# Two attention branches with a gate: a new layout table, later queueing of the local branch's value lists, and a shorter head

## The chip, the cores and the metric

The kernel runs on one core of one Trainium2 chip. The metric is the device time of one execution in microseconds; the time before is 808.96 us, the median of three runs (808.18 to 810.17). A core has five engines with queues of their own: TensorE (PE) multiplies, VectorE (DVE) and GpSimd (POOL) work on tiles, ScalarE (ACT) evaluates functions, and SyncE (SP) issues nearly all transfers here. PEld is TensorE's weight load.

## The reference

Both branches read the same x of 2048 tokens by 640, with 32 heads of 20. Branch A is full softmax attention, branch B attends to 8 positions at a distance of 2 (0, 2, ... 14 tokens back). A gate g per token mixes them.

```python
    def _A_ref(x, wqkv, wo):
        ...
        scores = jnp.einsum("bhqd,bhkd->bhqk", q, k) * scale
        p = _softmax(scores, axis=-1)
        o = jnp.einsum("bhqk,bhkd->bhqd", p, v)
        return (lambda x, *d: x.transpose(*d))(o, 0, 2, 1, 3).reshape(B, S, D) @ wo

    def _B_ref(x, wqkv, wo):
        ...
        W, dil = 8, 2
        ...
        logits = jnp.einsum("bhsd,bhswd->bhsw", q, kg) * scale
        logits = jnp.where(mask[None, None, :, :], logits, -1e9)
        attn = _softmax(logits, axis=-1)
        o = jnp.einsum("bhsw,bhswd->bhsd", attn, vg)
        ...
    x = A_x
    g = _sigmoid((x * gate_w).sum(-1, keepdims=True))
    a = _A_ref(x, A_wqkv, A_wo)
    b = _B_ref(x, B_wqkv, B_wo)
    return g * a + (1 - g) * b
```

## The kernel before

**Main work.** Branch A's scores are computed in units: one head, 128 keys, 512 queries. Four heads form a quad, and a quad with 512 queries is a group; there are 32 groups of 64 units, 2048 in all. PE writes a score tile of two or three units into one of two PSUM banks (line 1672), ACT takes the exponential of the whole tile (line 1697: `ebuf<-score`, 1024 or 1536 columns), and PE multiplies it with the values (line 1742, `obank<-ebuf,vA`). Of some tiles a further unit rides along: DVE turns it into an integer form (line 1687, `uD<-score`), adds three shifts to it (line 899, `eD<-uD`), and PE multiplies the four versions with scaled values (`obank<-uD,vA`, `obank<-eD,vS`). The exponentials of those units are so approximated without ACT: 408 of 2048 units ride, 1640 go through ACT. Each group is closed by a transpose on DVE (line 845, `oTt<-obank`), a division on GpSimd (lines 851 and 858) and a transfer into the layout of the output projection (line 864).

**Side work** goes through spare PSUM banks between the score tiles (helper `mm_group`, line 651): the value projection of A (`gen_v`, copies at line 814), the K and Q projections of the later quads (`gen_kq` in five parts f, `gen_q1` for the first quad), branch B in eight units u of 256 tokens (`gen_bproj` projects Q, K and V, line 945; `gen_b` forms the products and sums, lines 971, 981, 1068, 1078), and the output projection (`gen_fold`). K and Q of `gen_kq` go to the layout of the scores by transfers from `stg` (lines 703, 733, 756). For B, V's shifted windows are copied by four groups of four transfers, the value lists `vR` (line 953, `stage<-qkvB`), which the second product of `gen_b` reads (line 1068); the reciprocal goes through `rB` (lines 1054, 1056).

**The order is set while the program is built.** Every operation is handed to a planner (`T`, class `_Sched`) with an assumed duration and, for transfers, an assumed time to issue (`iss`, times `nd` transfers) and to land. The planner keeps a clock for each engine, and generators yield requests ("dve", "pe", "act", "bank", "cond") that it grants when its clocks allow. What comes out is a fixed order of instructions for each engine and semaphore waits between them; the assumed times are in no instruction, but they decide the order. Eighteen parameters of the planner are set again every few score tiles from the table `PLAN` (tile number to parameters, 138 rows): slack, thresholds for rides, priorities, and the target load of PE below which filler matmuls are put in (`filler`, line 1763).

**The head** ends with the first exponential. SyncE loads four quarters of x (`x_load`) and the weights. GpSimd makes an index ramp (line 536) and fills constants: V's ones (`vAones`, line 546), qT (line 563). DVE makes the identity from the ramp (lines 541, 542) and small constants. PE runs nine warm-up matmuls on zeros (line 548), turns the first quarter of x (line 1380), runs four more, and then alternates turns and K projections (line 1403); ACT and DVE copy the turned quarters out (lines 1393, 1396). GpSimd pads K's and Q's first weights (`w_pad`, line 617).

## Time and profile before

| what | us |
|---|---|
| median of three runs | 808.96 (808.18 to 810.17) |
| the profiled execution, its own time | 807.94 |
| its span, first to last instruction | 806.1 |
| first exponential starts | 19.28 |
| last exponential ends | 797.46 |
| ACT idle between those two | 17.5 |
| granted TensorE clock, mean | 0.999 |

The span is what the profile covers; 1.8 us lie around it. The first exponential ends the head, the last one starts the tail (final products, output projection, stores). Between them the table's idle time is where ACT had nothing to do. Engine busy times are unions: an instruction's duration overlaps the next one's, so mean durations are longer than what one more instruction costs. Transfers are all issued from SyncE's single queue except two stores at the end:

```profile
## 3 DMA queue, kind: packets, MB, share of 16 engines
q1 hardware_dynamic: 47124, 30.51, 15.6%
```

The transfer engines are 15.6% busy over the span, so their bandwidth is not short outside the head.

### The profile page before, as it was taken

Reading aid. Unit: us, or ns where it says so; the run is one execution under the profiler, and the core shown is the slowest. Engines: PE = TensorE matmul, PEld = TensorE weight load, DVE = VectorE, ACT = ScalarE, POOL = GpSimd, SP = SyncE. Lnnn points to the kernel's source line nnn. Section 1 sums busy time; section 2 is a strip of 40 time slices with the busy share of each in tenths; the row PEclk is TensorE's granted clock in tenths of the full one; section 3 lists DMA queues with packets and bytes.
Section 4 is the critical chain, followed back from the end, with each engine's and each line's share of the span. In section 5 each row is a group of like instructions: output and inputs, shape, how many; then the busy total and the mean of one; then the engine's idle time right before and its main releaser. Section 6 shows DMA issues by size and latency. Waiting matters only on the chain.

```text
span 806.1 us, 27829 instructions
## 1 busy us (share of the span) xinstructions
PE 746.2 (93%) x11855; PEld 280.5 (35%) x11857; DVE 741.8 (92%) x1266; ACT 769.8 (95%) x757; POOL 92.5 (11%) x148
## 2 busy tenths in 40 slices
PE   8999998989999898989999998989899999999997
PEld 4323342334334233323343342333234333333322
DVE  7878998989999999999999999999999899999896
ACT  4999999989999999999999999999999999999996
POOL 3010001110020010101110100100021010111110
PEclk9999999999999999999999999999999999999999
DMA  8001110141030021101301320310212003000001
GB/s 261 26 24 31 26 33 6 38 85 29 6 76 11 5 44 38 22 22 40 76 13 38 78 54 22 74 27 6 64 28 65 5 17 81 22 23 23 23 21 35
DMA packets 47535, 32.61 MB, mean 40 GB/s; under 512 B 15029, under 2 KB 45653, under 8 KB 47413
## 3 DMA queue, kind: packets, MB, share of 16 engines
q1 hardware_dynamic: 47124, 30.51, 15.6%
q8 instruction: 94, 1.54, 0.8%
q10 hardware_dynamic: 288, 0.33, 0.1%
q14 instruction: 29, 0.23, 0.1%
HBM read 9.34 MB, written 2.62 MB: 15 GB/s over the span
## 4 chain that ended last, share of the span: by engine, by line
DVE 35%; PE 29%; ACT 15%; issue 10%; SPq 7%; DMA 3%; POOL 0%; POOLq 0%; DVEq 0%; ACTq 0%
ACT ebuf L1697 15%; DVE uD L1687 12%; PE score L1672 8%; PE obank L1742 8%; DVE eD L899 8%; PE side L651 7%; SPq L953 6%; DVE stage L971 3%; PE score L651 3%; DVE qkvB L945 2%; DVE stage L1068 2%; DMA stage<-qkvB 2%; DVE oTt L845 1%; DVE vA L814 1%; DMA qT<-stg 1%
## 5 line engine op out<-in xcount | busy, mean ns | idle before, releaser
L1697 ACT ACTIVATE ebuf<-score 128x1024 bf16<-128x1024 f32 (+1 forms) x725 | 758.1, 1184 | 19.6 <-PE score L1672 17.8
L1672 PE MATMUL score<-qT,kT 32*128 32x512 bf16 x2048 | 285.7, 384 | 31.5 <-ACT ebuf L1697 20.7
L1687 DVE TENSOR_SCALAR uD<-score 128x512 int16<-128x512 f32 x408 | 269.9, 682 | 17.1 <-PE score L1672 16.0
L899 DVE TENSOR_SCALAR eD<-uD 128x2048 int16<-128x2048 int16 x306 | 209.6, 706 | 3.8 <-PE obank L1742 3.0
L1742 PE MATMUL obank<-ebuf,vA 128*21 128x512 bf16 x1640 | 153.2, 385 | 9.5 <-DVE oTt L845 3.4
L1672 PEld LDWEIGHTS score<-qT,kT 32*128 32x128 bf16 x2048 | 70.7, 91 | 262.2 <-ACT ebuf L1697 172.0
L1742 PE MATMUL obank<-eD,vS 128*21 128x512 bf16 x1224 | 107.7, 380 | 1.2 <-DVE eD L899 1.2
L651 PE MATMUL side<-xT,wBs 128*32 128x256 bf16 x2400 | 96.2, 281 | 1.7 <-DVE qkvB L945 1.2
L851 POOL TENSOR_TENSOR rcp<-rcp,gA 128x16 f32<-128x16 f32 x31 | 7.5, 243 | 659.6 <-DVE rcp L849 659.6
L651 PEld LDWEIGHTS side<-xT,wBs 128*32 128x32 bf16 x2400 | 68.4, 142 | 29.7 <-issue 14.5
L1742 PEld LDWEIGHTS obank<-ebuf,vA 128*21 128x21 bf16 x1640 | 36.7, 89 | 92.6 <-issue 57.5
L1068 DVE TENSOR_TENSOR stage<-stage,eB 128x2048 bf16<-128x2048 bf16 x40 | 48.0, 1224 | 6.2 <-DMA stage<-qkvB 6.2
L651 PE MATMUL side<-xT,WqP 128*32 128x512 bf16 (+2 forms) x605 | 48.5, 382 | 2.0 <-DVE qkvB L945 0.9
L971 DVE TENSOR_TENSOR stage<-qkvB 128x2048 bf16<-128x2048 bf16 x40 | 47.8, 1230 | 0.1
L945 DVE CAST qkvB<-side 128x512 bf16<-128x512 f32 (+1 forms) x72 | 42.1, 594 | 3.0 <-PE side L651 2.8
L1742 PE MATMUL obank<-uD,vA 128*21 128x512 bf16 x408 | 39.6, 379 | 0.0
L890 POOL TENSOR_TENSOR vS<-vA,vw 128x252 bf16<-128x252 bf16 x55 | 37.0, 693 | 19.1 <-DVE maskB L594 13.2
L1742 PEld LDWEIGHTS obank<-eD,vS 128*21 128x21 bf16 x1224 | 29.9, 91 | 21.2 <-DVE eD L899 4.0
L858 POOL TENSOR_TENSOR oN<-oTt,rcp 128x512 bf16<-128x512 f32 x31 | 32.7, 1054 | 2.4
L845 DVE STREAM_TRANSPOSE oTt<-obank 128x512 f32<-128x512 f32 x32 | 22.8, 712 | 4.8 <-PE obank L1742 4.6
L651 PE MATMUL side<-xT,oTd 128*32 128x512 bf16 (+1 forms) x500 | 26.1, 304 | 0.0
L651 PEld LDWEIGHTS side<-xT,WqP 128*32 128x32 bf16 (+2 forms) x605 | 13.1, 94 | 19.8 <-issue 7.9
(200 smaller groups left out, 477.0 us busy)
## 6 DMA issues: line engine op xcount, KB each, us to landing
stage<-qkvB SPq DMA_DIRECT2D x128, 80.6 KB, 2.1
wBs<-in_B_wqkv_dram SPq DMA_DIRECT2D x1, 2400.0 KB
kT<-stg SPq DMA_DIRECT2D x28, 80.0 KB
qT<-stg SPq DMA_DIRECT2D x28, 80.0 KB
oTd<-oN SPq DMA_DIRECT2D x108, 20.0 KB
out_dram<-outsb SPq DMA_DIRECT2D x12, 160.0 KB
oTd<-in_A_x_dram SPq DMA_DIRECT2D x2, 640.0 KB
WqP<-in_A_wqkv_dram SPq DMA_DIRECT2D x8, 150.0 KB, 2.5
```

Of the source, the lines that this page charges most:

```text
L651: ins = e.matmul(o[j:k, :], l(j) if callable(l) else l[:, j:k], r, start=(first and i == 0), stop=(last and i == n - 1), skip_group_check= ...
L858: T(en, c2, lambda e: e.tensor_tensor(oo, ii, ib, ALU.mult), reads=["rcp", "oTt"], writes=["oN0"])
L890: T("pool", 0.607, lambda e: e.tensor_tensor(vS[:, i, :, :], _ap(vA[q // 4], (kb * 4 + q % 4) * 4 * DV, [[0, K - 1], [1, 4 * DV]]), _ap(vw ...
L899: T("dve", 0.065 + 0.1334 * n, lambda e, k=k, sl=sl: e.tensor_scalar(eD[:, sl % NS, 0:512 * n].bitcast(I16), uD[d % NU][:, 0:512 * n].bitc ...
L945: t = TB(dvc(n * TOK), lambda e, o=o, i=i: e.tensor_copy(o, i), reads=[("side", b)], writes=[key])
L953: T("sp", 2.0 + 0.65 * 4, lambda e, w4=w4, lo=lo: [e.dma_start(vR[32 * w4:32 * w4 + 32, a * CN:(a + 1) * CN, :], vB[32 * a:32 * a + 32, :, ...
L971: TB(dvc(CH, 2), lambda e: e.tensor_tensor(o, i0, i1, ALU.mult), reads=["qB", "kB"], writes=[("prod", i)] + ([("WkP", 0)] if u == 0 else [ ...
L1068: TB(dvc(CH, 2), lambda e: e.tensor_tensor(o, i0, i1, ALU.mult), reads=["eB"] + [("vR", w4) for w4 in range(4)], writes=[("prod", i)], por ...
L1672: ins = e.matmul(o, kT[32 * j:32 * j + 32, q % NQS, kb * P:(kb + 1) * P], qT[32 * j:32 * j + 32, q % NQS, GROUPS[g][0] * 512:(GROUPS[g][0] ...
L1687: t = T("dve", 0.598, lambda e: e.tensor_scalar(uD[d % NU][:, 512 * i:512 * (i + 1)].bitcast(I16), side[x], UOFF, 0.0, op0=ALU.add, op1=AL ...
L1697: exps[s] = T("act", actc(512 * n), lambda e: e.activation(ebuf[s % NE][:, 0:512 * n], score[s % 2][:, 0:512 * n], ACTF.Exp, scale=LN2 / S ...
L1742: ins = e.matmul(obank[32 * j:32 * j + DV, :], v, src, start=(kb == 0), stop=(last and k >= len(lst) - 4), skip_group_check=True)
```

## The change

1. **B's value lists.** A new request `("sp", 0.4)` is granted only when SyncE's planned backlog is at most 0.4 us, and stands in front of each of the four list groups. The V part of unit u's projection waits until the lists of unit u - 1 are queued.
2. **Assumed times** of transfers: the lists land 3.2 + 4 x 0.65 us after the start of their issue (before 2.0 + 4 x 0.65), K's and Q's 2.7 + 0.765 n (2.2 + 0.65 n), the bounds' 2.4 + 0.55 n (2.2 + 0.65 n), the reciprocal's 2.4 + 0.65 n (2.0 + 0.5 n); B's output weights issue in the default time (3.7 before).
3. **K's first part** has weights of its own (`WkQ`, loaded in the head into `stage`), and may start once A's first value half and the second Q chunk are done; its Q part still waits for the last chunk. `gen_b` waits for that K part. `gen_q1` takes absolute values into `qbnd` instead of `stg`.
4. **The layout table** is new throughout: 140 rows.
5. **The head**: seven warm-up matmuls instead of nine, none behind the first turn (four before); the fills of V's ones stand behind GpSimd's second index ramp; the fills of qT wait for `ones2`.

```diff
-    0: ((0.31, 0.76), 0.01, 1.0, 5.5, 0.94, -1.37, -0.5, 9.99, 7.0, 5.87, 0.67, 0.62, 5.69, 4.3, 0.0, 0.63, 2, -3),
...
+    0: ((0.32, 0.64), 0.16, 2.5, 2.5, 0.94, -1.41, -0.97, 11.8, 7.0, 8.62, 0.67, 0.96, 4.4, 4.3, 0.0, 0.75, 2, -3),
+    5: ((0.32, 0.68), 0.38, 2.5, 1.0, 0.94, -1.48, -0.65, 11.8, 7.0, 7.05, 0.5, 0.53, 5.68, 4.3, 0.0, 0.51, 2, -3),
...
-    for i in range(2):
-        T("pool", 0.3, lambda e, i=i: e.memset(vA[i][:, :, :, :, 0:1], 1.0), writes=[("vAones", i)])
-
     warm_up = lambda e: e.matmul(obank[:, :], stg[:, 0:P], stg[:, 0:512], start=True, stop=True)
-    for i in range(9):
+    for i in range(7):
         T("pe", 0.43, warm_up, reads=[("stg", 0)], writes=["obank"])
...
-        T("pool", 0.95, lambda e, i=i: e.memset(qT[:, i, :].bitcast(FP32), 0.0), writes=[("qTz", i)])
+        T("pool", 0.95, lambda e, i=i: e.memset(qT[:, i, :].bitcast(FP32), 0.0), reads=["ones2"], writes=[("qTz", i)])
...
-              writes=[("woBp", f)] + ([("vA", kb, 0) for kb in range(KBN)] + [("vAones", 0)] if f == 0 else []), dma=True, iss=3.7)
+              writes=[("woBp", f)] + ([("vA", kb, 0) for kb in range(KBN)] + [("vAones", 0)] if f == 0 else []), dma=True)
...
+    WkQ = _ap(stage, 1024, [[DH * len(heads[0]), CN], [1, DH * len(heads[0])]])
+    T("sp", 3.0, lambda e: e.dma_start(WkQ, wA_v[:, :, D + DH * heads[0][0]:D + DH * heads[0][0] + DH * len(heads[0])]),
+      writes=["WkQ"], dma=True)
...
-        while not done.get(("q", POS[QCN - 1, 0])):
+        while not (done.get(("v", VORD[-1], 0)) and done.get(("q", POS[1, 0]))):
             yield ("cond",)
         for f in range(CN):
+            Wk, wk = (WkQ, ["WkQ"]) if f == 0 else (WqP, WQ)
...
-            T("sp", 2.2 + 0.65 * len(hs), lambda e, hs=hs: [e.dma_start(
+            T("sp", 2.7 + 0.765 * len(hs), lambda e, hs=hs: [e.dma_start(
...
+            done[("k", f)] = True
+            while not done.get(("q", POS[QCN - 1, 0])):
+                yield ("cond",)
...
-            T("sp", 2.2 + 0.65 * 4 * len(runs), lambda e, runs=runs, hs=hs: [e.dma_start(
+            T("sp", 2.4 + 0.55 * 4 * len(runs), lambda e, runs=runs, hs=hs: [e.dma_start(
...
-                w_load(1, 0)
+                w_load(0, 0)
             yield ("dve",)
             T("dve", dvc(512), lambda e, b=b, cols=cols: e.tensor_scalar(
-                stg[:, cols].bitcast(U16), side[b][:, :].bitcast(U16)[:, 1:1024:2], 0x7FFF, None, op0=ALU.bitwise_and),
-              reads=[("side", b)], writes=[("stg", qc)])
-            yield from mm_group(b, [(side[b][:, :], KM[0], stg[:, cols])], [("KM", 0), ("stg", qc)], mmc(512), first=False)
+                qbnd[:, :].bitcast(U16), side[b][:, :].bitcast(U16)[:, 1:1024:2], 0x7FFF, None, op0=ALU.bitwise_and),
+              reads=[("side", b)], writes=["qbnd"])
+            yield from mm_group(b, [(side[b][:, :], KM[0], qbnd[:, :])], [("KM", 0), "qbnd"], mmc(512), first=False)
...
+            while u and m == 2 and f0 == 0 and not done.get(("bproj", u - 1)):
+                yield ("cond",)
...
         for w4 in range(4):
+            yield ("sp", 0.4)
             lo = PADB - DIL - 2 * DIL * w4
-            T("sp", 2.0 + 0.65 * 4, lambda e, w4=w4, lo=lo: [e.dma_start(
+            T("sp", 3.2 + 0.65 * 4, lambda e, w4=w4, lo=lo: [e.dma_start(
...
-        while not (done.get(("bqk", u)) and (u == 0 or done.get(("bs", u - 1)))):
+        while not (done.get(("k", 0)) and done.get(("bqk", u)) and (u == 0 or done.get(("bs", u - 1)))):
...
-        T("sp", 2.0 + 0.5 * 4, lambda e: [e.dma_start(rB[0:32, j * TQ:(j + 1) * TQ], rQ[32 * j:32 * j + 32, :]) for j in range(4)],
+        T("sp", 2.4 + 0.65 * 4, lambda e: [e.dma_start(rB[0:32, j * TQ:(j + 1) * TQ], rQ[32 * j:32 * j + 32, :]) for j in range(4)],
...
+        elif req[0] == "sp":
+            if not force and sch.avail["sp"] > now + req[1]:
+                return False
...
     turn(0)
-    for i in range(4):
-        T("pe", 0.215, warm_up, reads=[("stg", 0)], writes=["obank"])
     x_out(0)
     T("pool", 0.8, w_pad(stage, 0, ebuf[3], 0, 4 * DH, 0), reads=[("ebuf", 3), "WkP"], writes=[("WkP", 0)])
     T("pool", 0.4, lambda e: e.iota(itmp2[:, :], [[-DH, 32]], base=0, channel_multiplier=1), writes=[("outsb", 0, 0)])
+    for i in range(2):
+        T("pool", 0.3, lambda e, i=i: e.memset(vA[i][:, :, :, :, 0:1], 1.0), writes=[("vAones", i)])
```

## The prediction

> **What bounds the kernel now.** I read the page's engine totals first, then ScalarE's (ACT's) instructions by form, its waits, the busy time by stretch, and last the timelines of the head and of one long wait.

> ```profile
> PE 746.2 (93%) x11855; PEld 280.5 (35%) x11857; DVE 741.8 (92%) x1266; ACT 769.8 (95%) x757; POOL 92.5 (11%) x148
> ```
> ```profile
> L1697 ACT ACTIVATE ebuf<-score 128x1024 bf16<-128x1024 f32 x533 | 512.6, 1072 | 13.1 <-PE score L1672 11.6
> L1697 ACT ACTIVATE ebuf<-score 128x1536 bf16<-128x1536 f32 x191 | 271.5, 1500 | 6.6 <-PE score L1672 6.2
> L1697 ACT ACTIVATE ebuf<-score 128x512 bf16<-128x512 f32 x1 | 0.6, 606 | 0.0
> ```
> Three engines stand above 92%. ACT's exponentials are nearly all its work, and ACT idles 19.7 us before them (13.1 + 6.6), 2.1 of it before the very first (19.28 us). The last one ends at 797.46, so the span of 806.1 is a head of 19.28, a stretch of 778.18 and a tail of 8.67 us; idle in the stretch is 17.5 us.

> ```profile
> ACT ebuf L1697 <- PE score L1672: 17.8, 29, 2.3
> ```
> Nearly all of it is a wait for score matmuls: PE is late with them. Where, the stretches show (PE, PEld, DVE, ACT, POOL busy):
> ```profile
> 40.00:60.00 20.00, 18.00 (x269) 5.85 (x269) 14.66 (x26) 17.69 (x19) 2.41 (x4) 1.00 0.10 24
> 100.00:150.00 50.00, 46.46 (x727) 17.27 (x728) 44.79 (x78) 47.14 (x49) 3.68 (x6) 1.00 0.11 23
> 150.00:200.00 50.00, 45.08 (x759) 18.26 (x747) 45.73 (x78) 47.27 (x47) 4.54 (x8) 1.00 0.26 57
> 250.00:300.00 50.00, 46.31 (x747) 18.00 (x745) 48.90 (x85) 50.00 (x53) 4.20 (x7) 1.00 0.07 16
> ```
> ACT is full from 250 to 300 us and loses 2.3, 2.9 and 2.7 us in the other three. The largest single loss, from the timelines of SyncE's queue, VectorE (DVE) and ACT:
> ```profile
> 169.81 2.55 SPq L953 DMA_DIRECT2D stage<-qkvB  x4
> 175.56 1.23 DVE L1068 TENSOR_TENSOR stage<-stage,eB 128x2048 bf16<-128x2048 bf16 x1 [2.69 <-DMA stage<-qkvB]
> 178.76 2.79 ACT L1697 ACTIVATE ebuf<-score 128x1536 bf16<-128x1536 f32 x2 [2.26 <-PE score L1672]
> ```
> The fourth value list of B is issued at 169.81 and in by about 175.5, 5.7 us later, where the planner had counted 2.0 + 4 x 0.65 = 4.6. DVE stands 2.69 us in front of the product that reads it, its next instruction is a transpose that frees PE's output bank, and ACT pays 2.26.

> **The change, part by part.**

> *Head.* Before:
> ```profile
> 1.10 3.20 DVE L541 CAST rB<-ebuf 128x128 f32<-128x128 int32 x1
> 1.22 4.02 PE L548 MATMUL obank<-stg 128*128 128x512 bf16 x9 [1.22 <-DVE stg L539]
> 5.41 1.57 PE L1380 MATMUL score<-ident,oTd 128*128 128x128 bf16 x20 [0.17 <-DVE eB L556]
> 6.83 1.03 PE L548 MATMUL obank<-stg 128*128 128x512 bf16 x4
> 7.69 1.28 PE L1380 MATMUL score<-ident,oTd 128*128 128x128 bf16 x20
> 19.28 1.45 ACT L1697 ACTIVATE ebuf<-score 128x1536 bf16<-128x1536 f32 x1 [2.09 <-PE score L1672]
> ```
> The cast takes 3.20 us beside GpSimd's fills (a smaller cast later, L571, takes 0.17), so the identity is ready at 5.26. With the fill of V's ones (2.36 us) moved back it will be ready about 3 us earlier, but the first quarter of x lands only at 5.05: gain at most 0.3. The four warm-ups behind the first turn cost 7.69 - 6.83 = 0.86. The second quarter lands at 6.96, so the second turn can begin at 7.0 in place of 7.69: 0.7 earlier. PE then runs turns and K projections back to back to 15.8 us; the next landings (9.19 and 11.09) are needed at about 9.3 and 11.5, just in time, so 0.7 reaches the first exponential. Bounds: 0 if a landing slips by as much, -0.9 with all of the 0.86. I take **-0.7**.

> The fills of qT now wait for DVE's small constants (ready near 3 us by the same rows without the stretched cast). Behind them on GpSimd stand 2.24 + 0.38 us of fills and the pad of K's weights, which started at 7.43 on a landing: 1.7 us of slack. The moved fill runs 8.1 to 10.4, in a gap that lasts to 11.59 (pad of Q's weights, again on a landing); V's first copy needs it at 18.71. Nothing is paid; without that cover the pad would pass it on, at most 2.4 us. The extra weight load for the first K part (issue 0.39 us, as the WqP loads) goes out on SyncE between 8.4 and 13.39, when that queue only waited; B's weights behind it are in at 23 and first read near 100 us. The absolute values of Q now go through qbnd: the same three instructions of 0.69, one buffer, gated by V's projection as before. Nothing.

> Fewer warm-ups have a price the head's rows show: their starts are 0.43 us apart while the four later ones take 0.22, and the first turn ran 1.57 against 1.28. PE's pace doubled inside it, near 6.07 us (starts 0.107 apart, then 0.056). Seven of them end near 4.2, and PE idles 0.9 before the first turn. [...] Rival 1 works the row out.

> *ScalarE's work.* Counted in the built programs, exponentials go from 533, 191 and 1 (1024, 1536, 512 columns) to 543, 186 and 0: 1644 units of 512 in place of 1640; four score tiles less ride on DVE (408 to 404, with three shifts less, 306 to 303: some 4 x 0.61 + 3 x 0.63 = 4.3 us of DVE work gone, which is slack and not on the path). The three forms' busy sums (784.7) overlap into 758.1 for the line, a factor 0.966; one costs 0.929, 1.373 and 0.585. So 10 x 0.929 - 5 x 1.373 - 0.585 = **+1.8**. This lies on the engine that sets the end. Bounds: +1.5 to +2.1 by the choice of the factor.

> *Tail.* The last output group closes with four shifted products more behind the last exponential's: 4 x 107.7/1224 = 0.35 us, of which I take **+0.2** (0 to +0.4).

> *B's value lists.* Each of the four list transfers is queued only when SyncE's backlog is under 0.4 us, and 5.8 us instead of 4.6 are counted until it is in; the reciprocal's lists get 5.0 and 4.35 for 4.0 and 3.5, K's and Q's 7.3 for 6.1. No instruction is added; what stands in DVE's order behind a list moves later.
> ```profile
> DVE stage L1068 <- DMA stage<-qkvB: 6.2, 6, 2.7
> ```
> DVE waits six times on lists, 6.2 us, and 1.0 on Q's lists. ACT's idle within five us behind these waits: 2.26, 0.81, 0.34, 0.32, 0.30, 0.27, 0.20, 0.17, 0.14, in all 4.8. The first is certain to come from the list; for the rest PE and DVE had other late work. So -2.3 to -4.8, and I take **-3.5**. The page gives 2.1 us from one list DMA's issue to its landing.
> [...]

> *The new table.* It moves work between stretches. By the 150th exponential the kernel before has done 339 units and beside them 380 of B's projection matmuls, 380 of V's and 64 of B's sums; the changed one 324 units beside 280, 360 and 40, with 76 rides in both. At 96.2/2400 = 0.040, 0.050 and 0.047 us each PE sheds 4.0 + 1.0 + 1.1, and for 15 units 15 x (285.7/2048 + 153.2/1640) = 3.5 more, about 9.6 us; ACT sheds 15 x 0.465 = 7.0. PE gains 2.6 us on ACT there, where ACT idled 5.1 us that I have not counted yet (40.7 to 127 us). Between 0 and -5.1, I take the 2.6, rounded to **-2.5**. The B work put off comes at units 440 to 660, where PE was 45 to 47 of 50 us busy: room, but no longer slack.

> Sum: -0.7 + 1.8 + 0.2 - 3.5 - 2.5 = **-4.7 us**. The profiled execution took 807.94 (806.1 of span and 1.8 around it), 1.0 under the median of 808.96; the difference goes on the median: **804.3 us**.

> **The rivals.**
> 1. *The clock rises late.* Before, 4.85 us passed from the first warm-up (1.22) to the doubling (6.07). If the gap of 0.9 us makes that count begin anew at 5.1, it comes at 9.95. At half pace a turn takes 2.1 and a K projection 2.1, for 1.1 each: the second turn ends at 9.4 and the first K projection near 10.75, where the chain of before had it at 10.05. So +0.7 in place of -0.7: 804.3 + 1.4 = 805.7. Bounds: no delay, -0.7; cold to the chain's end, 7 such pieces at 1.0 more, +7. Against it: PE is active for 3.0 us before the gap and again from 5.1. [...]
> 2. *Waits only move.* With three engines above 92%, what is taken from one wait is met by the next late one: lists and table bring nothing, -0.7 + 1.8 + 0.2 = +1.3, 810.3. For it: DVE idles only 64 us in the span. Against it: ACT runs 250 to 300 us without a gap.
> 3. *The held lists starve DVE* (slower). SyncE issues at 0.65 to 0.75 us a DMA, an output list or a K list takes 3 to 4.6 us; a list that waits for a short backlog goes out behind them, and each of B's eight units ends on it. In half of them ACT pays the 2.26 of 178.76: 9.0 in place of 4.8, so +4.2 for -3.5: 804.3 + 7.7 = 812.0. The other terms are -1.2, so the kernel is slower than before from 6.0 us of such idle on, by over 0.3% from 8.4. For it: the first unit's lists now stand behind Q's second list on SyncE. Against it: the planner puts other work in front of a late list.
> 4. *The table removes most waits.* Two thirds of the 17.5 go: -11.7 + 1.3 = -10.4, 798.6. For it: PE's sum beside ACT's falls in the first third. Against it: ACT's idle at 543 us (1.60) and after 600 comes from no list.

> **How the numbers follow.** Chances: forecast 0.36, rivals 0.10, 0.16, 0.24, 0.14. 0.3% of 808.96 is 2.4 us, about what a measurement tells from no change: faster is below 806.5, slower above 811.4. The forecast's own range is 801 to 808 (head 0 to -0.9, work +1.5 to +2.1, lists -2.3 to -4.8, table 0 to -5.1): faster 0.29, same 0.06, slower 0.01. Rival 1 gives 0.06 and 0.04, rival 2 0.01, 0.10 and 0.05 slower, rival 3 0.03 same and 0.21 slower, rival 4 0.14 faster. Sums: 0.50, 0.23, 0.27. The range 798 to 814 takes in the rivals' centres and leaves rival 3's upper end and a better rival 4 outside.

> **What would show it.** First exponential at 18.6 (above 19.3: rival 1, with warm-up-paced turns after 7 us). DVE's wait on value lists under 2 us, no ACT wait of 2 us near a list (over 8 us: rival 3). ACT's gaps before 130 us about half. ACT's gaps in all 11 to 12; if they stay at 17, rival 2. The forecast is wrong if the gain is there while ACT's gaps are not smaller, or if the tail grows by over a microsecond.

## The result and the profile after

The changed kernel took 801.75 us (median of 4, 799.44 to 803.49), the kernel before on the same chip 809.57 (median of 4); the ratio is 0.9898, 95% interval [0.9872, 0.9923]. It is faster, by 7.8 us where 4.7 were forecast; 804.3 us was the number, 798 to 814 the range. The profiled execution took 802.39, of which 800.5 is its span. (The layout table has 132 rows in the kernel before and 134 in the changed one.)

The engine totals of the changed kernel, its exponentials by form (busy us and mean ns, then ACT's idle time before them), and the waits of ACT and DVE that the prediction named:

```profile
PE 751.9 (94%) x11875; PEld 282.2 (35%) x11875; DVE 735.0 (92%) x1259; ACT 770.6 (96%) x761; POOL 91.8 (11%) x147
```
```profile
L1709 ACT ACTIVATE ebuf<-score 128x1024 bf16<-128x1024 f32 x543 | 520.6, 1065 | 7.7 <-PE score L1684 6.5
L1709 ACT ACTIVATE ebuf<-score 128x1536 bf16<-128x1536 f32 x186 | 264.6, 1497 | 4.5 <-PE score L1684 4.2
```
```profile
ACT ebuf L1709 <- PE score L1684: 10.7, 23, 2.1
```
```profile
DVE stage L1077 <- DMA stage<-qkvB: 0.4, 1, 0.4
```

ACT still sets the end and PE is still what it waits for, but the waits fell from 17.8 us (29 times) to 10.7 (23), and DVE's waits on B's value lists from 6.2 us to 0.4. The same stretches as before. Each row has the window, its length, busy us and (instructions) of PE, PEld, DVE, ACT and POOL, then the granted clock, the share of the DMA engines and GB/s:

```profile
40.00:60.00 20.00, 19.50 (x271) 5.78 (x270) 13.77 (x25) 19.34 (x23) 1.27 (x2) 1.00 0.10 27
100.00:150.00 50.00, 46.88 (x690) 16.33 (x686) 48.39 (x85) 49.62 (x51) 4.70 (x7) 1.00 0.08 19
150.00:200.00 50.00, 48.11 (x792) 19.10 (x793) 47.47 (x82) 49.67 (x51) 6.83 (x11) 1.00 0.22 49
250.00:300.00 50.00, 47.72 (x850) 20.28 (x842) 47.56 (x78) 49.45 (x53) 3.97 (x7) 1.00 0.16 35
```

ACT loses 0.7, 0.4 and 0.3 us in the three stretches where it had lost 2.3, 2.9 and 2.7. Between 250 and 300, where nothing had been lost, it now loses 0.5 us; that this is B's work, put off to later, was not followed up. The head is the part that went the other way (timeline; in brackets the idle time before an instruction and what ended it):

```profile
1.10 0.23 DVE L543 CAST rB<-ebuf 128x128 f32<-128x128 int32 x1
...
1.22 3.17 PE L547 MATMUL obank<-stg 128*128 128x512 bf16 x7 [1.22 <-DVE stg L541]
5.22 4.30 PE L1392 MATMUL score<-ident,oTd 128*128 128x128 bf16 x40 [0.84 <-DMA oTd<-in_A_x_dram]
...
19.84 1.45 ACT L1709 ACTIVATE ebuf<-score 128x1536 bf16<-128x1536 f32 x1 [2.09 <-PE score L1684]
```

The cast is 0.23 us instead of 3.20 now that GpSimd's fill is not beside it (with the old head under the new body, oldhead below, it takes 3.20 again), and the turns start 0.19 us earlier; but the two turns take 4.30 us for 40 transposes, 0.107 apart, so PE ran at its low pace almost to the end of both. The trace's record of the granted clock has the doubling at 9.24 us (before: 6.07). The first exponential is 0.55 us later than before instead of 0.7 earlier.

### The profile page after: what moved, and what is told of

The parts are those of the page before. It is cut to its first block, busy times and chain, and to the rows that moved or that the text cites. A ratio compares the mean times of both kernels' runs of the same rounds, so it can differ in the third digit from the quotient of the medians.

```text
span 800.5 us, 27853 instructions
## 1 busy us (share of the span) xinstructions
PE 751.9 (94%) x11875; PEld 282.2 (35%) x11875; DVE 735.0 (92%) x1259; ACT 770.6 (96%) x761; POOL 91.8 (11%) x147
## 4 chain that ended last, share of the span: by engine, by line
PE 43%; DVE 28%; ACT 16%; issue 10%; SPq 2%; DMA 1%; POOL 0%; DVEq 0%; ACTq 0%
ACT ebuf L1709 15%; PE score L1684 13%; PE obank L1754 12%; PE side L650 11%; DVE uD L1699 8%; DVE eD L905 6%; PE score L650 3%; DVE stage L980 3%; DVE stage L1077 2%; DVE qkvB L953 2%; SPq L962 1%; DVE oTt L851 1%; PE score L1392 1%; PE side L1087 1%; DVE stg L734 1%
## 5 line engine op out<-in xcount | busy, mean ns | idle before, releaser
L1709 ACT ACTIVATE ebuf<-score 128x1024 bf16<-128x1024 f32 (+1 forms) x729 | 758.8, 1175 | 12.2 <-PE score L1684 10.7
L1684 PE MATMUL score<-qT,kT 32*128 32x512 bf16 x2048 | 288.3, 385 | 27.5 <-ACT ebuf L1709 19.7
L1699 DVE TENSOR_SCALAR uD<-score 128x512 int16<-128x512 f32 x404 | 266.6, 680 | 19.1 <-PE score L1684 18.8
L905 DVE TENSOR_SCALAR eD<-uD 128x2048 int16<-128x2048 int16 x303 | 206.2, 706 | 3.5 <-PE obank L1754 2.8
L1754 PE MATMUL obank<-ebuf,vA 128*21 128x512 bf16 x1644 | 156.0, 386 | 2.3 <-DVE oTt L851 0.8
L1754 PE MATMUL obank<-eD,vS 128*21 128x512 bf16 x1212 | 105.9, 381 | 0.7 <-DVE eD L905 0.7
L650 PEld LDWEIGHTS side<-xT,wBs 128*32 128x32 bf16 x2340 | 67.8, 142 | 33.4 <-issue 15.8
L650 PE MATMUL side<-xT,WqP 128*32 128x512 bf16 (+2 forms) x550 | 44.4, 382 | 1.8 <-DVE stg L701 0.8
L953 DVE CAST qkvB<-side 128x512 bf16<-128x512 f32 (+1 forms) x70 | 41.0, 595 | 2.9 <-PE side L650 2.7
L1754 PEld LDWEIGHTS obank<-eD,vS 128*21 128x21 bf16 x1212 | 29.6, 91 | 18.2 <-issue 2.0
L650 PE MATMUL score<-WvH,xT 128*32 128x320 bf16 x400 | 21.0, 301 | 0.0
```

The source lines that it names most:

```text
L650: ins = e.matmul(o[j:k, :], l(j) if callable(l) else l[:, j:k], r, start=(first and i == 0), stop=(last and i == n - 1), skip_group_check= ...
L905: T("dve", 0.065 + 0.1334 * n, lambda e, k=k, sl=sl: e.tensor_scalar(eD[:, sl % NS, 0:512 * n].bitcast(I16), uD[d % NU][:, 0:512 * n].bitc ...
L953: t = TB(dvc(n * TOK), lambda e, o=o, i=i: e.tensor_copy(o, i), reads=[("side", b)], writes=[key])
L1684: ins = e.matmul(o, kT[32 * j:32 * j + 32, q % NQS, kb * P:(kb + 1) * P], qT[32 * j:32 * j + 32, q % NQS, GROUPS[g][0] * 512:(GROUPS[g][0] ...
L1699: t = T("dve", 0.598, lambda e: e.tensor_scalar(uD[d % NU][:, 512 * i:512 * (i + 1)].bitcast(I16), side[x], UOFF, 0.0, op0=ALU.add, op1=AL ...
L1709: exps[s] = T("act", actc(512 * n), lambda e: e.activation(ebuf[s % NE][:, 0:512 * n], score[s % 2][:, 0:512 * n], ACTF.Exp, scale=LN2 / S ...
```

## The experiments

Twelve runs follow: eleven changed kernels, and the kernel after once more. Kernels were measured in several sets, each with runs of before beside them, and a ratio is to before in the same set. "Gaps" is ACT's idle time between the first exponential's start and the last one's end, and "work" what is left of that stretch; both, like the first exponential and the doubling of the clock, are from one profiled execution each. Two rows show the kernels that are compared.

| kernel | median us (runs) | ratio to before, interval | clock doubles | first exp. | work | gaps |
|---|---|---|---|---|---|---|
| before | 809.57 (4) | | 6.07 | 19.28 | 760.6 | 17.5 |
| after | 801.75 (4) | 0.9898 [0.9872, 0.9923] | 9.24 | 19.84 | 761.4 | 10.4 |
| nine | 800.76 (5) | 0.9896 [0.9877, 0.9915] | 5.88 | 18.73 | 760.9 | 9.5 |
| oldhead | 800.96 (5) | 0.9899 [0.9879, 0.9918] | 5.78 | 19.14 | 760.9 | 9.1 |
| after_again | 801.32 (6) | 0.9912 [0.9887, 0.9937] | 4.29 | 18.76 | 761.1 | 10.0 |
| one_warm | 802.83 (6) | 0.9922 [0.9897, 0.9947] | 9.44 | 19.87 | 761.1 | 11.4 |
| before_newhead | 809.43 (12) | 1.0003 [0.9984, 1.0022] | 4.84 | 18.53 | 760.3 | 20.8 |
| before_nine | 810.01 (12) | 1.0019 [1.0000, 1.0038] | 4.51 | 18.90 | 760.7 | 20.3 |
| land31 | 822.85 (4) | 1.0177 [1.0142, 1.0212] | 5.57 | 18.52 | 765.4 | 24.2 |
| land20 | 825.24 (4) | 1.0207 [1.0176, 1.0238] | 4.49 | 18.62 | 766.7 | 29.6 |
| nohold | 828.58 (4) | 1.0284 [1.0241, 1.0326] | 4.87 | 18.59 | 776.5 | 21.9 |
| after_oldtable | 847.22 (4) | 1.0511 [1.0474, 1.0549] | 4.06 | 18.76 | 774.3 | 42.0 |
| before_newtable | 866.38 (4) | 1.0741 [1.0703, 1.0779] | 5.17 | 18.98 | 775.4 | 61.5 |
| before_held | 931.69 (4) | 1.1549 [1.1502, 1.1595] | 6.71 | 19.59 | 763.7 | 139.8 |

### The head: four kernels under one body or the other

*nine*: the kernel after with two warm-ups more.

```diff
-    for i in range(7):
+    for i in range(9):
         T("pe", 0.43, warm_up, reads=[("stg", 0)], writes=["obank"])
```

> The kernel after with nine warm-up matmuls instead of seven; nothing else moves on any engine. Theory 1 (the clock): seven warm-ups end at 4.39 us, TensorE then idles 0.84 us, and the granted clock doubles only at 9.24 us. Nine last about 0.9 us longer, so TensorE has no gap before the first x quarter (landed 5.05 to 5.18 us); the clock doubles between 5.8 and 6.2 us, as in the kernel before (6.07), most of the first forty transposes take 0.05 instead of 0.107 us, and the first exponential starts between 18.5 and 19.3 us instead of 19.84. Nothing behind that gains or loses, so the time is 0.5 to 1.3 us below the kernel after, 800.4 to 801.2. Theory 2 (the late clock in that one execution was chance, or what paces the head is the landing of x and the weights): first exponential at 19.8 us, time 801.7. Theory 3 (nine warm-ups only delay the turns by what they last): first exponential at 20.3 us, 802.2.

*oldhead*: the body of after under the head of before (9 + 4 warm-ups, V's ones in front, qT's fills without their wait; the planner gives the four no time, so that the order behind stays that of after).

```diff
+    for i in range(2):
+        T("pool", 0.3, lambda e, i=i: e.memset(vA[i][:, :, :, :, 0:1], 1.0), writes=[("vAones", i)])
-    for i in range(7):
+    for i in range(9):
...
+    for i in range(4):
+        T("pe", 0.0, warm_up, reads=[("stg", 0)], writes=["obank"])
-    for i in range(2):
-        T("pool", 0.3, lambda e, i=i: e.memset(vA[i][:, :, :, :, 0:1], 1.0), writes=[("vAones", i)])
```

> The body of the kernel after (lists, table, assumed times, weights) under the head of the kernel before: nine warm-ups, four more between the first two turns, the fill of V's ones ahead of the indices. The order behind the head is that of the kernel after. Theory 1: the head of the change costs 0.55 us, so this one is 0.55 us faster than the kernel after: first exponential at 19.28 us, clock doubled at about 6.1 us, time 801.2. Theory 2 (the head does not reach the end): 801.7 whatever the first exponential does. If the head had been worth the predicted 0.7 us, the time would be 802.5.

*before_newhead* and *before_nine*: the body of before under the new head, with seven and with nine warm-ups (the planner's clock of PE is moved on by the 0.86 us of the four that are gone, and the seven are planned as long as nine, so that the order behind stays; qT's fills wait as in after).

```diff
-    for i in range(2):
-        T("pool", 0.3, lambda e, i=i: e.memset(vA[i][:, :, :, :, 0:1], 1.0), writes=[("vAones", i)])
-    for i in range(9):
+    for i in range(7):
...
-    for i in range(4):
-        T("pe", 0.215, warm_up, reads=[("stg", 0)], writes=["obank"])
+    sch.avail["pe"] += 0.86
+    for i in range(2):
+        T("pool", 0.3, lambda e, i=i: e.memset(vA[i][:, :, :, :, 0:1], 1.0), writes=[("vAones", i)])
```

> The kernel before with the new head alone: seven warm-ups, none between the turns, the fill of V's ones behind the indices; order of everything behind it that of the kernel before. Theory 1 (clock rises late again, near 9.2 us): first exponential at 19.84 instead of 19.28 us, time 0.55 us above the kernel before, 810.1 against 809.6. As predicted for the head: first exponential at 18.6 us, 0.7 us below, 808.9.

> The kernel before with the new head, but nine warm-ups ahead of the turns and none between them. Theory 1: TensorE is busy without a gap to the first turn, the clock doubles at about 6.1 us, and the four warm-ups that are gone from between the turns (0.86 us cold, 0.43 at the full clock) no longer delay the second: first exponential between 18.5 and 19.3 us, time 0 to 0.8 us below the kernel before, 808.8 to 809.6. Theory 2 (landings pace the head): as the kernel before with its new head and as the kernel before, within 0.2 us of both.

With nine, the clock doubled at 5.88 us and the first exponential came at 18.73, as theory 1 had it, at 800.76 us. But the same seven warm-ups that were late under the body of after were early under the body of before: clock at 4.84 us, first exponential at 18.53, theory 1 of that kernel wrong and the number of the prediction (18.6) met. So the late doubling need not belong to the kernel; the next runs show that it belongs to an execution. And the head reaches the end only weakly: oldhead is as fast as nine, and both kernels with the old body are no faster than before (809.43 and 810.01 against 808.58 for before in that set), although their first exponential came 0.4 to 0.75 earlier. A gain of 0.5 us is below what these intervals (0.4% wide) can show. The four warm-ups between the turns cost 0.86 us at the doubled clock in before (6.83 to 7.69, with the doubling at 6.07); the expectation of before_nine has that figure as the cold one and 0.43 for the full clock, which no run shows.

### The phase of the clock: the same kernel again, and one warm-up

*after_again* is the kernel after, unchanged. *one_warm* is after with one warm-up.

```diff
-    for i in range(7):
-        T("pe", 0.43, warm_up, reads=[("stg", 0)], writes=["obank"])
+    for i in range(1):
+        T("pe", 3.01, warm_up, reads=[("stg", 0)], writes=["obank"])
```

> The kernel after once more, unchanged, for the phase of the clock. Theory (the granted clock is decided in stretches of 3.413 us whose grid lies at another place in every execution): the clock doubles either at 4.1 to 4.9 us, with the first exponential at 18.5 to 18.8 us as in the kernel before under the new head, or at 8.3 to 11 us with 19.7 to 20.3 us; the times of the rounds fall with the mean granted clock by 0.4 to 0.7 us for each 0.001, as in the runs of the other kernels, and the line reaches 799.5 to 800.5 us at a clock of 0.999. Rival (the head of the change always costs 0.55 us): clock at 9.2 us, first exponential at 19.84 us again.

> The kernel after with one warm-up matmul instead of seven, the order behind it unchanged. Theory (a stretch of 3.413 us must be nearly full of matmuls before the clock doubles, and seven warm-ups fill one only at some phases): with one, no stretch before the first turn at 5.1 us is full at any phase, so the clock doubles between 8.5 and 12 us, the first exponential starts at 19.7 to 20.6 us, and the time is 0.3 to 1.3 us above that of nine warm-ups and 0 to 0.7 above seven. Rival (warm-ups do nothing that reaches the end): the time of the kernel after, first exponential at 18.6 us or so.

The head of after_again and then of one_warm, from the timeline:

```profile
1.22 3.17 PE L547 MATMUL obank<-stg 128*128 128x512 bf16 x7 [1.22 <-DVE stg L541]
5.09 1.29 PE L1392 MATMUL score<-ident,oTd 128*128 128x128 bf16 x20 [0.70 <-DMA oTd<-in_A_x_dram]
6.97 1.29 PE L1392 MATMUL score<-ident,oTd 128*128 128x128 bf16 x20 [0.59 <-DMA oTd<-in_A_x_dram]
...
18.76 1.45 ACT L1709 ACTIVATE ebuf<-score 128x1536 bf16<-128x1536 f32 x1 [2.09 <-PE score L1684]
```
```profile
1.22 0.61 PE L547 MATMUL obank<-stg 128*128 128x512 bf16 x1 [1.22 <-DVE stg L541]
5.09 4.45 PE L1392 MATMUL score<-ident,oTd 128*128 128x128 bf16 x40 [3.27 <-DMA oTd<-in_A_x_dram]
...
19.87 1.45 ACT L1709 ACTIVATE ebuf<-score 128x1536 bf16<-128x1536 f32 x1 [2.09 <-PE score L1684]
```

Instruction for instruction the first is the kernel after, and its second turn starts at 6.97 us, when its x lands, as the prediction had it (7.0): the clock doubled at 4.29 us. The rival "always 0.55 us" is out. The six runs take 0.91 us longer for each 0.001 that the mean granted clock falls, steeper than the 0.4 to 0.7 expected; their line reaches 800.1 at 0.999, as expected. One warm-up puts 0.61 us of work in front of the turns. Of the stretch from 2.61 to 6.03 us PE was busy 0.94 of 3.42, of the next one 3.41 of 3.41; at its end, 9.44 us, the clock doubled, and the first exponential came at 19.87, where it was expected. Over the seven executions with seven warm-ups the doubling came at 4.06 to 5.57 us in six (first exponential 18.52 to 18.76) and at 9.24 in the one that the result shows. The time of one_warm, 802.83, is 1.5 us above after_again, more than the 0 to 0.7 expected, with intervals that overlap. That the late start reaches the end is not shown.

### The hold, the table and the assumed times

*nohold*: after without the request; *after_oldtable*: after with the rows of PLAN of before; *before_newtable*: before with the rows of after; *before_held*: before with the request alone.

```diff
 nohold
         for w4 in range(4):
-            yield ("sp", 0.4)
             lo = PADB - DIL - 2 * DIL * w4
 after_oldtable
-PLAN = {0: ((0.32, 0.64), 0.16, ...
+PLAN = {0: ((0.31, 0.76), 0.01, ...
 before_newtable
-PLAN = {0: ((0.31, 0.76), 0.01, ...
+PLAN = {0: ((0.32, 0.64), 0.16, ...
 before_held
         for w4 in range(4):
+            yield ("sp", 0.4)
             lo = PADB - DIL - 2 * DIL * w4
...
+        elif req[0] == "sp":
+            if not force and sch.avail["sp"] > now + req[1]:
+                return False
```

> The kernel after without the condition that B's value lists are queued only at a backlog of SyncE under 0.4 us; all assumed times, the table, the head and the weight loads stay. Theory 1 (the hold is what keeps the lists out of other transfers' way): VectorE's waits on B's lists return from 0.4 towards the 6.2 us of the kernel before, ScalarE's gaps grow by 2 to 3.5 us, time 803.5 to 805.5. Theory 2 (the longer assumed landing, 3.2 instead of 2.0 us, already moves VectorE's work behind the lists, so the hold does nothing): VectorE's waits on lists stay under 1.5 us, time within 1 us of the kernel after, 801 to 802.5. Theory 3 (holding the lists costs more than it gives): below 800.5.

> The kernel after with the layout table of the kernel before. Theory 1 (the table is worth the 2.5 us of the prediction, the rest comes from lists, times and weights): time 803.5 to 805, ScalarE's gaps 13 instead of 10.4 us. Theory 2 (a table fits only the assumed times for which it was searched; with other times it is a random draw): ScalarE's gaps over 16 us, time above 807, so that the new times with the old table are no better than the kernel before. Theory 3 (the table is worth nothing): 801 to 802.5.

> The kernel before with the new layout table alone. Theory 1 (table and code add up): 2.5 us below the kernel before, 806 to 807, with VectorE's waits on B's lists still near 6 us. Theory 2 (a table fits only the assumed times for which it was searched): at or above the kernel before, ScalarE's gaps over 18 us.

> The kernel before with the hold of B's lists alone (its own table, times, weight loads and head). Theory 1 (the hold takes away VectorE's waits on lists, whatever the table): waits on lists under 2 instead of 6.2 us, ScalarE's gaps 1 to 3.5 us shorter, time 805.5 to 808. Theory 2 (the hold only moves the waits, or spoils the fit of the table): waits on lists 4 us or more or ScalarE's gaps no shorter, time at or above the kernel before.

No theory that named a size had it: +27 us without the hold and +46 with the old table under the new code (against the 801.3 of after_again, from another set), +60 with the new table and +125 with the hold under the old code (against the 806.61 that before took in this set). What held are the theories without an upper end: that a table fits only its own assumed times (both tables), and that the hold alone moves the waits or spoils the fit (before_held). For nohold no theory had the time; its waits are those of theory 2. The waits on lists, which the hold was thought to remove, answered by themselves. DVE's wait on lists without the hold, then before with the hold, then before with the new table:

```profile
DVE stage L1076 <- DMA stage<-qkvB: 0.2, 1, 0.2
```
```profile
DVE stage L1069 <- DMA stage<-qkvB: 15.8, 4, 12.0
```
```profile
DVE stage L1070 <- DMA stage<-qkvB: 1.2, 2, 0.8
```

Without the hold they stay away, with the hold alone they more than double, and with the new table alone, which has neither the hold nor the longer assumed landing, they fall from 6.2 to 1.2 us, where "still near 6 us" was expected of a table that adds up. Where the 27 us of nohold went, against nine (execution against execution: 825.8 - 798.1 = 27.7 us): 15.6 to more work of ACT and 12.3 to its gaps. The forms and waits of nohold, and for comparison the riding units of after:

```profile
L1698 DVE TENSOR_SCALAR uD<-score 128x512 int16<-128x512 f32 x374 | 248.2, 679 | 41.7 <-PE score L1683 41.1
```
```profile
ACT ebuf L1708 <- PE score L1683: 22.6, 37, 2.3
```
```profile
L1699 DVE TENSOR_SCALAR uD<-score 128x512 int16<-128x512 f32 x404 | 266.6, 680 | 19.1 <-PE score L1684 18.8
```

DVE stands 41 us in front of score matmuls instead of 19, and 30 units fewer ride; each is 512 columns more for ACT, 0.466 us at the 0.931 that 1024 columns take from one start to the next, 14.0 in all. So most of the loss goes with the planner's other order and not with a wait for a transfer. In before_held it is larger still: in the table of stretches (columns as above) ACT has hardly any work for a tenth of the span.

```profile
480.00:500.00 20.00, 8.43 (x119) 2.51 (x115) 11.32 (x14) 6.98 (x7) 0.00 (x0) 0.79 0.21 49
500.00:520.00 20.00, 13.03 (x284) 8.93 (x280) 11.66 (x19) 0.82 (x2) 0.26 (x1) 0.62 0.04 11
520.00:540.00 20.00, 3.04 (x56) 0.90 (x48) 6.49 (x7) 0.00 (x0) 1.31 (x1) 0.64 0.34 73
540.00:560.00 20.00, 11.54 (x276) 7.92 (x272) 13.39 (x20) 0.14 (x1) 0.26 (x1) 0.67 0.01 2
560.00:580.00 20.00, 12.48 (x416) 11.72 (x408) 6.63 (x12) 0.68 (x2) 0.26 (x1) 0.84 0.33 70
```

From 487 to 586 us work of B runs with no score tile between; ACT has only two units' small exponentials there (three gaps of ACT: 29.0, 42.7 and 25.5 us, the first two in front of B's exponentials). In the second gap DVE waits 12.0 us for lists. Why the planner set so much of B ahead of the next score tile was not followed up.

### A control for the fit of the table

*land31* changes an assumed time by 0.1 us, *land20* puts it back to the value of before.

```diff
-            T("sp", 3.2 + 0.65 * 4, lambda e, w4=w4, lo=lo: [e.dma_start(
+            T("sp", 3.1 + 0.65 * 4, lambda e, w4=w4, lo=lo: [e.dma_start(
 land20
+            T("sp", 2.0 + 0.65 * 4, lambda e, w4=w4, lo=lo: [e.dma_start(
```

> A control: the kernel after with the assumed landing of B's lists at 3.1 instead of 3.2 us, a difference that says nothing about the chip; the order is that of the kernel after up to the 368th of 729 exponentials and another one behind. Theory (the layout table was searched for one exact set of assumed times, and any other order is a draw that costs several us): time 805 to 830, gaps of ScalarE over 15 us, fewer exponential tiles on VectorE than 404. Then the 27 us that the kernel without the hold lost are not the price of the hold. Rival (the plan is smooth, and the hold itself was worth 27 us): within 1.5 us of the kernel after.

> The kernel after with the assumed landing of B's lists at 2.0 us again, as in the kernel before, but with the hold; the order is that of the kernel after up to the 359th of 729 exponentials. Theory 1 (it is the longer assumed landing that took VectorE's waits on B's lists away; without the hold they stayed at 0.2 us): the waits behind the 359th exponential return, 1.5 to 4 us in this half, and the time is 805 to 830 as for any other order. Theory 2 (the hold alone takes them away): waits under 0.8 us, time as for any other order.

A tenth of a microsecond in a number that stands in no instruction cost 21.5 us (822.85 against 801.32), though the engines' orders agree up to the 368th exponential. The kernel without the hold parts from after at the 175th and loses 27, land20 at the 359th and loses 24. So 27 us is of the size that two other changes of the order cost under this table, one of them a change without a meaning, and the price of the hold cannot be read from it. In land20 one wait on a list of 1.4 us came back, which is under the 1.5 to 4 expected and over the 0.8 of the rival: undecided.

## Why the prediction was right, and where it was not

**What bounds the kernel.** ACT at 96% and PE's late score matmuls: confirmed in the kernel after, whose gaps are mostly waits for scores. It does not hold for every kernel here: half of before_held's idle time of ACT (71.6 us) stands in front of B's exponentials.

**Head, -0.7: for the first exponential wrong in the profiled execution (+0.55) and about right in the six others with seven warm-ups; in the time it was not seen.** The step that failed is "the second quarter lands at 6.96, so the second turn can begin at 7.0": it held in after_again, whose first turn ran at the doubled clock (20 transposes in 1.29 us), and not in after, where 40 took 4.30. In the six others the first exponential came at 18.52 to 18.76; the four executions with the old head lie at 18.98 to 19.59, so the size of the gain hangs on the executions compared. The kernel before under the new head took as long as before (1.0003 [0.9984, 1.0022]), which neither shows nor excludes 0.7 us.

Rival 1's sign, a first exponential above 19.3 behind turns at the warm-ups' pace, was there in the profiled execution, but as a draw. The clock's records have the later changes at whole multiples of 3.413 us from the first: 63 and 64 of them in after (9.24, then 224.28 and 227.69 us), 64 in after_again (4.29, then 222.74), 234 in before (6.07, then 804.79). The place of that grid differs between executions. In after a stretch ran from 2.41 to 5.82 us; PE was busy 2.57 of it, and the next one stayed slow. In after_again one ran from 0.87 to 4.29, busy 3.07, and the clock rose. Rival 1's price (+0.7 for 0.55) was about right, its working was not: it counted 4.85 us from the end of the gap, and the doubling came 4.02 us behind it in after (5.22 to 9.24) and 4.35 in one_warm (5.09 to 9.44), each time at the end of a stretch that, counted back on the grid, was full (PE busy 3.42 of 3.42 and 3.41 of 3.41). That the grid runs already before the first doubling is an inference from these rows. Its chance of 0.10 stands beside one execution in seven. Nine warm-ups instead of seven close the gap in front of the turns (in nine they run from 1.22 to 5.24 us, and the turns start at 5.18); nine is the version with the lowest median, but no interval sets it apart from after.

**ACT's work, +1.8: measured +0.74.** The term was mis-sized. The counts were right (10 narrow tiles more, 5 wide and one of 512 fewer), but from one start to the next, listed gaps left out, a narrow one took 0.9312 us instead of 0.9331: 505.65 - 497.32 = +8.33 for the narrow ones, -6.71 and -0.61 for the others, -0.27 for small ones. At before's prices it would have been near +1.8. Why an exponential came 2 ns sooner was not followed up.

**Tail, +0.2:** +0.24.

**Lists, -3.5, and table, -2.5:** ACT's gaps shrank by 7.1 (7.5 in after_again), the sum of 6.0 nearly right. By place, 4.1 of the 7.1 lie before 130 us (6.4 in before, 2.3 in after; "about half" was the sign), where no value list has been issued yet (the first goes out at 160.98 us in before), and the rest behind. So what the prediction put on the table in that stretch, 2.5, was too small, and what is left for the lists is at most 3.1. The single largest loss, 2.26 us behind a list, is gone: after's longest gap is 0.98.

By part of the change the split cannot be read: both terms were worked out as if each part kept its value without the other. The gaps before 130 us are 2.3 in nohold too, and 10.6 and 10.5 in after_oldtable and before_newtable, so there it is table and code together that count, and the hold does not. What took the waits on lists away stays open. They are gone in nohold, which has the longer assumed landing, and nearly gone in before_newtable, which has neither that nor the hold; another order alone can do it. What can be said is that code, assumed times and table give -7 together, and that each pairing that was tried without one of them was 27 to 60 us worse than the kernel it was made from, the hold alone 125.

**The sum.** In the profiled pair head, work, tail and gaps add up to +0.55 + 0.74 + 0.24 - 7.14 = -5.6 us, which is what the span fell by. The medians lie 7.8 apart. The rest is of the size of the scatter: before's profiled execution, 807.94, was below all four of its timed runs (808.18 to 811.38). So the forecast of 4.7 came close to the 5.6 by errors that offset each other: the head 1.25 too good, the work 1.1 too dear, the gaps 1.1 too small. Added up, the bounds of the terms give 799.7 to 809.2, wider than the 801 to 808 that the prediction calls the forecast's own range.

**Rivals.** Rival 2 (waits only move) would have left 17 us of gaps: out. Rival 3 (held lists starve DVE) did not happen in after, and before_held shows that the danger was real, at 125 us rather than 7.7 and in another place than the one that was priced. Rival 4 asked for 11.7 us fewer gaps and 798.6; gaps fell by 7 to 8.

**Half-clock stretches, a term that the sum did not have.** In the middle of after the granted clock falls to a half for one stretch. Busy time by stretches of the grid, after and then nine at the same work (windows within 0.1 us of its grid):

```profile
217.45:220.86 3.41, 3.36 (x54) 1.29 (x46) 3.11 (x7) 3.41 (x5) 1.05 (x2) 1.00 0.00 0
220.86:224.28 3.42, 2.58 (x25) 0.60 (x22) 3.28 (x8) 3.42 (x5) 2.27 (x5) 1.00 0.02 5
224.28:227.69 3.41, 3.41 (x52) 1.04 (x50) 2.76 (x5) 2.51 (x4) 0.00 (x0) 0.50 0.07 17
227.69:231.10 3.41, 3.15 (x55) 1.30 (x52) 3.20 (x7) 3.27 (x4) 0.00 (x0) 1.00 0.04 9
```
```profile
217.60:221.00 3.40, 3.03 (x36) 0.88 (x33) 3.22 (x8) 3.40 (x5) 2.60 (x5) 1.00 0.02 5
221.00:224.40 3.40, 2.87 (x31) 0.67 (x32) 3.38 (x7) 3.40 (x5) 0.73 (x2) 1.00 0.02 6
224.40:227.80 3.40, 2.92 (x68) 1.24 (x64) 3.37 (x7) 3.40 (x5) 0.00 (x0) 1.00 0.07 18
```

The granted clock (behind POOL) is 1.00, 1.00, 0.50 and 1.00 in after. The stretch from 220.86 is thin on PE (2.58 of 3.42); in the next one, at half clock, ACT loses 0.90 us. In nine the same work is cut elsewhere by the grid (PE busy 2.87 to 3.03 of 3.40), the granted clock stays at 1.00 and ACT is full. The same spot dropped again in after_again, at 222.74 us. The granted clock is also what much of the scatter goes with: in 41 runs of before the time rises by 0.71 us for each 0.001 that the mean granted clock falls (correlation -0.83), in 26 runs of the five kernels with the body of after by 0.78 (-0.87). The mean clocks were 0.9960 and 0.9977; at 0.75 us for each 0.001 about 1.3 us of the 6.7 between their mean times (808.14 and 801.43) goes along with the clock. That is an association and no cause shown: a thin stretch is itself a loss, and the profiled execution of before had no such drop in its middle (the only one is at 804.79 us, in its last 1.3 us) while that of after had one.

## What to carry to other kernels

A table that was searched under one set of assumed times is one object with that code: price the pair, don't add its parts, and before reading an ablation as the worth of what was left out, run one with a change that means nothing. Let warm-up matmuls last until the first real work: with a gap of 0.6 to 0.8 us the clock doubled at 4.06 to 5.57 us in six executions and at 9.24 in one (counted back on the grid, a stretch began at 0.65 to 2.16 us in the six, at 2.41 in the one); without one, or with 0.2 us, it doubled at 4.51 to 6.71 in six. One profile is one draw of that grid, so compare a step of a microsecond over several executions, and look at the granted clock first.
